# A linear-attention state without zero blocks, its products on 64x64 parts of the array, and a new order of all engines

## The chip, the cores and the metric

The kernel runs on one core of one Trainium2 chip. The metric is the device time of one execution in microseconds (us); lower is better. The engines have names in the profile: PE is TensorE's matmul and PEld its weight load, DVE is VectorE, ACT is ScalarE, POOL is GpSimd, and SP issues the transfers (DMA). Each engine works through its own queue in the order in which the program gave it its instructions, and waits for others by semaphores. TensorE writes into PSUM, which only VectorE and ScalarE read.

## The reference

Two layers. The first is a linear attention with a decaying state, over 4 batches, 8 heads, 768 time steps and a head size of 48; the second is a dense layer with a squared ReLU in its middle, on 3072 tokens of width 384 with a hidden width of 2048.

```python
state = zeros(B, H, D, D)
for t in range(S):
    cur = einsum('bhd,bhe->bhde', u[None] * k[t], v[t])
    y[t] = einsum('bhd,bhde->bhe', r[t], state + cur)
    state = w[t][..., None] * state + einsum('bhd,bhe->bhde', k[t], v[t])
x = y as (3072, 384)
out = (maximum(x @ w_in, 0) ** 2) @ w_out
```

All inputs and the output are in 32-bit floats; w lies between 0.80 and 0.95.

## The kernel before

Time is cut into 12 steps of 256 tokens, three for each batch (`NB = 3`). A step has two chunks c of 128 tokens, and the 128 partitions hold pairs of tokens: rows `c * 64` to `c * 64 + 63` are chunk c, and j = 0 or 1 is the token of a pair. Heads go in four pairs p, with e = 0 or 1 the head of a pair; a head's 48 columns are padded to 64 in the operands of transposes, so that head e of a pair lies on partitions `e * 64` on.

The work of one step s, by the names that the order uses:

- `ld.s.w`, `.r`, `.k`, `.v` load one step's inputs (384 KB each), `ld.g.i` and `ld.g.o` a quarter of w_in and w_out (768 KB each), which `cast.i.g` and `cast.o.g` turn into 16-bit floats.
- `ww_`, `lw_` (logarithm), `cum_` (cumulative sums by a matmul with a triangle), `exp_` give the decays; `ac_` the decay over a whole chunk. `rw_`, `kw_`, `rd_` apply them to r and k.
- `tr_` and `rkt_` transpose these through TensorE and PSUM (steps 0 to 2), `dtr_` by a transposing transfer (steps 3 to 11), into `rkT`.
- `p_` multiplies k and r of the same chunk, `pm_` masks the result.
- `ku_`, `qp_`, `q_`, `vq_` form the term with u, token by token.
- `su_` adds up the chunk's outer products of k and v in PSUM (the state update), `ts_` adds the old state S to it, `sn_` multiplies by the decay and gives the new S.
- `y_` (masked products with v), `yq_` (the term with u) and `yc_` (r with the carried state S) add into one PSUM tile of two banks, bank c for chunk c. `ysb_` copies it out; `yt_` and `xt_` (steps 0 to 3) or `dyt_` (a transposing transfer, steps 4 to 11) turn it into xT.
- `m1_` is x @ w_in in eight groups of six matmuls, `rl_` the ReLU, `sq_` the square. For steps 0 to 4 `m2_` multiplies by w_out in four quarters for each chunk. Steps 5 to 11 use a form with seven products in place of eight: `sw_` and `tw_` add and subtract blocks, `pw_` are the seven products, `cx_` and `ow_` combine them. `os_` scales, `store` writes.

Nothing schedules this but one text, `ORDER` (lines 17 to 91): a list of words, each one operation of one step, executed in that order (lines 638 to 650), so that each engine's queue is the order of its words. A letter behind = says which engine does it (V is DVE, A is ACT, G is POOL), a number behind a colon which PSUM tile it uses. Buffers come from small pools and are free for the next step after a counted number of uses (`uses_of`, `buf`). `warm_` are matmuls on zeros that keep TensorE at work in the opening.

In the state tile S and in PSUM each head pair takes 96 columns on all 128 partitions: rows of head e times columns of both heads. Only the block with the same head is wanted. The other block is computed by `su_` (its matmul takes the weights of both heads and the v of both heads) and is multiplied away in `sn_`, since `ac_` is held with a zero for it: the tile is cleared once (line 275), and two activations fill in each half (lines 360 and 361). So S is zero off the head's own block, and `yc_` can contract over all 128 partitions in one matmul.

The lines that matter: L408 `p_`, L430 `su_`, L438 and L440 `ts_`, L444 `sn_`, L454 the matmuls of `y_`, `yq_` and `yc_` (all issued by `y_mm`), L360 `ac_`, L517 `m1_`, L540 `m2_`, L594 `pw_`, L225 `cast`, L336 to L340 `cum_`.

## Time and profile before

| what | us |
| --- | --- |
| runs | 178.8, 177.38, 178.2 |
| median | 178.2 |
| span of the profiled execution, first to last instruction | 176.7 |
| PE busy in the span | 168.7 |
| DVE busy | 141.4 |
| ACT busy | 135.7 |
| POOL busy | 125.8 |

Of the profiled execution the page gives the span; what the device time holds beyond it is not listed. The page gives busy time, share and number of instructions of each engine, then the busy share over 40 slices of the span as digits (9 is 90% or more). A chain of waits follows the work that ended last back to the start: "DMA" in it is a transfer that was waited for, "SPq" the issuing of transfers, "issue" time without a visible reason. In groups, a row gives line, engine, operation, tiles and shape, the count, then busy us and mean ns of one, then the idle time of the engine before it and what ended that. For a matmul "64*128" is the part of the array that it uses, rows by columns. Matmuls overlap, so a mean duration is longer than the time from one start to the next. In a timeline the columns are start, length and what.

### The profile page before, as it was taken

Reading aid. Unit: us, or ns where it says so; the run is one execution under the profiler, and the core shown is the slowest. Engines: PE = TensorE matmul, PEld = TensorE weight load, DVE = VectorE, ACT = ScalarE, POOL = GpSimd, SP = SyncE. Lnnn points to the kernel's source line nnn. Section 1 sums busy time; section 2 is a strip of 40 time slices with the busy share of each in tenths; the row PEclk is TensorE's granted clock in tenths of the full one; section 3 lists DMA queues with packets and bytes.
Section 4 is the critical chain, followed back from the end, with each engine's and each line's share of the span. In section 5 each row is a group of like instructions: output and inputs, shape, how many; then the busy total and the mean of one; then the engine's idle time right before and its main releaser. Section 6 shows DMA issues by size and latency. Waiting matters only on the chain.

```text
span 176.7 us, 5829 instructions
## 1 busy us (share of the span) xinstructions
PE 168.7 (95%) x2431; PEld 133.3 (75%) x2431; DVE 141.4 (80%) x221; ACT 135.7 (77%) x229; POOL 125.8 (71%) x116
## 2 busy tenths in 40 slices
PE   7969799999999999999999999999999999999993
PEld 2336678866687677578776888889988888989992
DVE  5299976994888968997877979979899879788731
ACT  5677799998659896939899799997897688477320
POOL 6298979999978099969999319759939665165220
DMA  5999999999699999797999959989959930330123
GB/s 142 315 305 340 380 244 347 370 347 254 152 220 240 287 199 254 184 215 179 308 225 194 329 136 222 224 113 269 251 115 132 227 53 4 108 114 4 45 93 134
DMA packets 82667, 36.55 MB, mean 207 GB/s; under 512 B 75857, under 2 KB 81106, under 8 KB 82642
## 3 DMA queue, kind: packets, MB, share of 16 engines
q1 hardware_dynamic: 82642, 36.19, 82.7%
q8 instruction: 19, 0.31, 0.7%
q14 instruction: 6, 0.05, 0.1%
HBM read 25.17 MB, written 4.72 MB: 169 GB/s over the span
## 4 chain that ended last, share of the span: by engine, by line
PE 85%; SPq 6%; DMA 5%; issue 1%; ACT 1%; ACTq 0%
PE one L517 35%; PE one L594 19%; PE one L540 15%; PE att L454 7%; DMA w_st_b<-in_moe_w_in_dram 5%; SPq L205 4%; PE att L408 3%; PE att L430 2%; SPq L213 2%; PE att L338 1%; SPq L233 1%; PE one L500 1%; PE att L340 1%; PE one L383 1%; PE att L336 0%
## 5 line engine op out<-in xcount | busy, mean ns | idle before, releaser
L517 PE MATMUL one<-xT_b,wi_sb 128*128 128x256 bf16 x576 | 70.3, 273 | 0.6 <-ACT gt_b L524 0.4
L517 PEld LDWEIGHTS <-wi_sb 128*128 128x128 f16 x576 | 54.7, 98 | 9.4 <-issue 1.3
L524 ACT ACTIVATE gt_b<-one 128x512 f16<-128x512 f32 x70 | 40.8, 596 | 10.1 <-PE one L517 9.4
L532 ACT ACTIVATE gt_b<-gt_b 128x1024 bf16<-128x1024 f16 x42 | 43.5, 1056 | 1.4 <-DVE gt_b L526 1.0
L419 DVE TENSOR_TENSOR pmT_b<-att,mask 128x1024 bf16<-128x1024 f32 x22 | 26.3, 1217 | 4.2 <-PE att L408 4.2
L540 PE MATMUL one<-wo_sb,gt_b 128*128 128x384 f16 x160 | 28.7, 326 | 0.0
L594 PEld LDWEIGHTS <-gt_b 128*128 128x128 bf16 x280 | 23.2, 98 | 0.9 <-issue 0.4
L311 POOL TENSOR_TENSOR ku_b<-k_b,u_bc 128x768 f32<-128x768 f32 x12 | 22.3, 1862 | 1.0 <-ACT ac_buf L360 0.8
L316 POOL TENSOR_TENSOR ku_b<-ku_b,r_b 128x768 f32<-128x768 f32 x12 | 22.2, 1848 | 0.6 <-DMA r_b<-in_r_dram 0.4
L540 PEld LDWEIGHTS <-gt_b 128*128 128x128 bf16 x160 | 15.1, 98 | 9.6 <-issue 0.5
L444 POOL TENSOR_TENSOR S_b<-t_b,ac_buf 128x384 bf16<-128x384 f32 x20 | 16.9, 846 | 5.4 <-ACT t_b L438 4.8
L526 DVE TENSOR_SCALAR gt_b<-one 128x512 f16<-128x512 f32 x26 | 17.6, 686 | 3.0 <-PE one L517 2.2
L322 POOL TENSOR_TENSOR vq_b<-v_b,q_b 128x768 bf16<-128x768 f32 x12 | 18.2, 1518 | 0.9 <-DVE q_b L319 0.8
L594 PE MATMUL one<-wo_sb,gt_b 128*128 128x192 f16 x168 | 16.2, 246 | 0.0
L374 DVE TENSOR_TENSOR rdec_buf<-r_b,att 128x768 bf16<-128x768 f32 x12 | 11.4, 948 | 1.8 <-POOL r_b L304 0.8
L374 DVE TENSOR_TENSOR rdec_buf<-k_b,att 128x768 bf16<-128x768 f32 x12 | 11.4, 948 | 1.7 <-ACT ac_buf L360 1.1
L319 DVE TENSOR_REDUCE q_b<-ku_b 128x16 f32<-128x768 f32 x12 | 11.3, 944 | 1.7 <-POOL ku_b L316 1.7
L599 ACT ACTIVATE w_st_b<-one 128x192 f32<-128x192 f32 x14 | 4.4, 329 | 10.3 <-PE one L594 10.2
L304 POOL TENSOR_TENSOR r_b<-r_b,w_b 128x384 f32<-128x384 f32 x8 | 8.1, 1014 | 4.7 <-DMA r_b<-in_r_dram 4.7
L292 POOL TENSOR_TENSOR ww_b<-w_b 128x384 f32<-128x384 f32 x7 | 8.0, 1149 | 4.5 <-DMA w_b<-in_w_dram 4.5
L594 PE MATMUL one<-w_st_b,gt_b 128*128 128x192 f16 x112 | 11.2, 246 | 0.0
L440 DVE TENSOR_TENSOR t_b<-S_b,att 128x384 f32<-128x384 bf16 x16 | 8.8, 548 | 2.9 <-POOL S_b L444 2.8
(100 smaller groups left out, 266.5 us busy)
## 6 DMA issues: line engine op xcount, KB each, us to landing
w_b<-in_w_dram SPq DMA_DIRECT2D x12, 384.0 KB, 5.9
r_b<-in_r_dram SPq DMA_DIRECT2D x12, 384.0 KB, 5.4
k_b<-in_k_dram SPq DMA_DIRECT2D x12, 384.0 KB, 5.3
v_b<-in_v_dram SPq DMA_DIRECT2D x12, 384.0 KB, 5.0
out_dram<-w_st_b SPq DMA_DIRECT2D x23, 192.0 KB, 2.2
w_st_b<-in_moe_w_in_dram SPq DMA_DIRECT2D x4, 768.0 KB, 9.5
w_st_b<-in_moe_w_out_dram SPq DMA_DIRECT2D x4, 768.0 KB, 9.1
rkT_b<-rdec_buf SPq DMA_TRANSPOSE x18, 3.5
```

The costliest lines, as they stand in the source:

```text
L311: nc.gpsimd.tensor_mul(buf("ku", s)[:], buf("k", s)[:, :, 1:3, :], u_bc[:, :, None, :].to_broadcast([C, H, 2, D]))
L316: nc.gpsimd.tensor_mul(ku[:], ku[:], buf("r", s)[:, :, 0:2, :])
L322: nc.gpsimd.tensor_mul(buf("vq", s)[:].rearrange("p j h d -> p h j d"), buf("v", s)[:], buf("q", s)[:, :, :, None].to_broadcast([C, H, 2, D]))
L374: nc.vector.tensor_mul(rdec[:, i, :, heads, 0:D], x.rearrange("p h j d -> p j h d"), decay[:, None, :, :].to_broadcast([C, 2, n, D]))
L419: nc.vector.tensor_mul(pmT, ps_p[:].rearrange("p e (a x) -> p (e a) x", a=2), mk.to_broadcast([C, 4, 2 * C]))
L444: nc.gpsimd.tensor_mul(buf("S", s + c, 1 - c)[:], buf("t", s, c)[:].rearrange("p (a e d) -> p a e d", a=HP, e=2), tiles["a_c", s][:, :, c, ...
L517: nc.tensor.matmul(ps1[:, j, :], wi_sb[:, n // 4, kk, n % 4 * 128:(n % 4 + 1) * 128], xT[:, :, kk, :], start=(kk == 0), stop=(kk == KT - 1))
L524: nc.scalar.activation(rl, m1, AF.Relu, scale=RS)
L526: nc.vector.tensor_scalar(out=rl, in0=m1, scalar1=RS, scalar2=0.0, op0=ALU.mult, op1=ALU.max)
L532: nc.scalar.activation(gt, rl, AF.Square)
L540: nc.tensor.matmul(m2, gt[:, n, c * C:(c + 1) * C], wo_sb[:, n, :], start=(n == 0), stop=(n == NT - 1))
L594: nc.tensor.matmul(where_to, gt[:, n, :], wo[:, n, :], start=(n == 0 and i in (1, 2, 5)), stop=(n == NT // 2 - 1), skip_group_check=True)
```

## The change

The state S loses its zero blocks: it is [128, 4, 48] in place of [128, 4, 2, 48], rows e of a pair holding head e alone. `ts_`, `sn_` and the decay tile of `ac_` shrink to that size; `ac_` is one activation, and the clearing of its tile goes.

`su_` issues a matmul for each head e, with 64 rows (chunk c) and 64 columns (head e) of the array, writing 48 columns to partitions `e * 64` on. The carried product can no longer contract over 128 partitions: each head's matmul uses the 64 rows of its e. It is split in halves. `yc_` does the heads with c = e, `yb_` the others, so that within a half each row part of the array writes another PSUM bank. Between the halves stands other work whose matmuls use another part size of the array; in steps 0 and 1 `yd_` takes the second half with 64x32 parts.

The order is new as a whole, for all engines; `ku_`, `qp_`, `vq_` and `sn_` may run on DVE, and in step 0 `rd_`, `tr_`, `rkt_`, `ysb_`, `yt_` and `xt_` come in halves. The diff, cut to its core; of the order only the opening and the end:

```diff
 ORDER = """
-ld.0.w warm_.10.1 ld.1.w ld.0.u ld.0.r ld.0.k ld.1.k ww_.0=V lw_.0 ld.1.r cum_.0:1 ww_.1=V ub_:1 lw_.1 exp_.0 ld.0.v
-rw_.0=G ac_.0 warm_.1.3 uc_=A cum_.1:0 ld.0.i kw_.0=V warm_.4.3 ku_.0 ac_.1 rd_.0.0 exp_.1 ld.1.v rd_.0.1 tr_.0.0:0
-rkt_.0.0=A kw_.1=V ld.1.i tr_.0.1:1 rw_.1=G rd_.1.1 warm_.4.2 ld.2.i rkt_.0.1=A ld.3.i qp_.0 warm_.1.0 rd_.1.0 v_.0=A
-ld.2.w p_.0.0:n pm_.0.0 su_.0:1 tr_.1.1:2 ts_.0.0=A q_.0 p_.0.1:0 rkt_.1.1=A sn_.0.0 warm_.4.0 pm_.0.1 ld.2.k
...
+ld.0.k ld.0.w ww_.0=V warm_.6.1 ld.0.u ld.0.r ld.1.w warm_.3.1 lw_.0 kw_.0=G ld.1.k ub_:3 ld.1.r uc_=V cum_.0:0
+ku_.0=V warm_.4.2 ld.0.v exp_.0 rw_.0=V rd_.0.1.1 tr_.0.1.1:1 rkt_.0.1.1=A qp_.0=G ld.1.v rd_.0.0.1 tr_.0.0.1:0 ld.2.w
+rkt_.0.0.1=A warm_.4.2 ww_.1=G rd_.0.1.0 rd_.0.0.0 p_.0.1:1 ac_.0 ld.2.i kw_.1=G q_.0 tr_.0.1.0:2 lw_.1 tr_.0.0.0:0
+cum_.1:0 pm_.0.1 rw_.1=G warm_.1.1 warm_.8.3 ld.1.i ld.0.i rkt_.0.1.0=A ac_.1 ku_.1=V ld.3.i vq_.0=G exp_.1 ld.2.k
+v_.0=A rd_.1.0 rkt_.0.0.0=A su_.0:1 ld.2.r p_.0.0:n ts_.0.0=A tr_.1.0:3 rd_.1.1 v_.1=A sn_.0.0=G qp_.1=G rkt_.1.0=A
+tr_.1.1:2 yd_.0:0 yq_.0 rkt_.1.1=A pm_.0.0 q_.1 ts_.0.1=V y_.0 yc_.0 cast.i.2=G ysb_.0.0=A p_.1.1:n ysb_.0.1=A
+yt_.0.0:3 xt_.0.0=A yt_.0.1:2 pm_.1.1 sn_.0.1=G ww_.2=G p_.1.0:0 su_.1:1 xt_.0.1=A cast.i.1=A m1_.0.5:3 m1_.0.4:0
+pm_.1.0 vq_.1=G lw_.2 ts_.1.0=V m1_.0.2:1 rl_.0.5=A sn_.1.0=V cum_.2:0 rl_.0.4=A m1_.0.3:3 ts_.1.1=V rl_.0.2=A exp_.2
+ld.2.v sn_.1.1=V y_.1:1 rl_.0.3=A yq_.1 yc_.1 yd_.1 cast.i.0=V ld.0.o m1_.0.1:2 ysb_.1=A cast.i.3=V m1_.0.0:3
...
+sw_.10.1.3=G sq_.11.0=A sw_.9.1.4=V sw_.9.0.4=V cx_.10.1=V pw_.9.7 pw_.9.3 pw_.10.6 sw_.11.1.1=V ow_.10.1=V sq_.11.1=A
+ow_.9.4=V pw_.9.4 ow_.9.2=V sw_.10.1.4=V sw_.10.0.4=V ow_.9.3=A cx_.10.2=A store.9.0 store.3.0 pw_.10.5 sw_.11.1.2=G
+store.9.1 sw_.11.0.1=G pw_.11.1:0 pw_.11.2:3 cx_.10.3=A sw_.11.1.4=V cx_.11.1=A pw_.10.7 pw_.10.3 ow_.11.1=V
+ow_.10.2=V store.10.0 sw_.11.0.3=G sw_.11.0.2=G pw_.11.6 sw_.11.1.3=G ow_.10.4=V pw_.11.5 cx_.11.2=A sw_.11.0.4=G
+pw_.10.4 cx_.11.3=V pw_.11.7 ow_.10.3=V store.10.1 pw_.11.3 ow_.11.4=V pw_.11.4 store.11.1.1 ow_.11.2=V store.11.0
+warm_.1.5 ow_.11.3=V store.11.1.0
 """
...
-        rkT=(2, [C, 2, 2, HP, C], BF16), pmT=(2, [C, 2, 4, 2, C], BF16), t=(2, [C, DM], FP32),
-        S=(6, [C, HP, 2, D], BF16), y_sb=(2, [C, 2, DM], BF16), xT=(4, [C, 2, KT, C], BF16),
+        rkT=(2, [C, 2, 2, HP, C], BF16), pmT=(2, [C, 2, 4, 2, C], BF16), t=(2, [C, HP * D], FP32),
+        S=(6, [C, HP, D], BF16), y_sb=(2, [C, 2, DM], BF16), xT=(4, [C, 2, KT, C], BF16),
...
-        for e in range(2):
-            rows = slice(e * DP, (e + 1) * DP)
-            nc.scalar.activation(
-                a_c[rows, :, :, e], cs[rows, 0, DM:DM + 2 * HP].rearrange("p (a c) -> p a c", c=2), AF.Exp)
+        nc.scalar.activation(a_c[:], cs[:, 0, DM:DM + 2 * HP].rearrange("p (a c) -> p a c", c=2), AF.Exp)
...
         for j in range(2):
             for p in range(HP):
-                for c in range(n_c):
-                    part = slice(c * Q, (c + 1) * Q)
-                    nc.tensor.matmul(ps_su[c][:, p * 2 * D:(p + 1) * 2 * D],
-                                     rdec[part, 1, j, 2 * p:2 * p + 2, :], v_bf[part, 2 * p:2 * p + 2, j, :],
-                                     start=(j == 0 and p == 0), stop=(j == 1), skip_group_check=True)
+                for e in range(2):
+                    for c in range(n_c):
+                        part = slice(c * Q, (c + 1) * Q)
+                        nc.tensor.matmul(ps_su[c][e * DP:(e + 1) * DP, p * D:(p + 1) * D],
+                                         rdec[part, 1, j, 2 * p + e, :], v_bf[part, 2 * p + e, j, :],
+                                         start=(j == 0 and p == 0), stop=(j == 1), skip_group_check=True)
...
-        nc.gpsimd.tensor_mul(buf("S", s + c, 1 - c)[:],
-                             buf("t", s, c)[:].rearrange("p (a e d) -> p a e d", a=HP, e=2),
-                             tiles["a_c", s][:, :, c, :, None].to_broadcast([C, HP, 2, D]))
+        product("sn_", s, c)(buf("S", s + c, 1 - c)[:],
+                             buf("t", s, c)[:].rearrange("p (a d) -> p a d", a=HP),
+                             tiles["a_c", s][:, :, c, None].to_broadcast([C, HP, D]))
...
+    def carried(s, swap, size):
+        rkT, first = buf("rkT", s), 0 if s % NB else 1
+        S = {c: buf("S", s, c) for c in range(first, 2)}
+        for p in range(HP):
+            for j in range(2):
+                for e in range(2):
+                    c, rows, h = e ^ swap, slice(e * DP, (e + 1) * DP), 2 * p + e
+                    if c in S:
+                        for at in range(0, Q, size):
+                            y_mm(s, c, slice(h * D, (h + 1) * D),
+                                 rkT[rows, 0, j, p, c * Q + at:c * Q + at + size], S[c][rows, p, :], j, at)
...
     def yc_(s):
-        rkT = buf("rkT", s)
-        for c in range(0 if s % NB else 1, 2):
-            S_c = buf("S", s, c)
-            for p in range(HP):
-                for j in range(2):
-                    y_mm(s, c, slice(2 * p * D, (2 * p + 2) * D), rkT[:, 0, j, p, c * Q:(c + 1) * Q],
-                         S_c[:, p].rearrange("p e d -> p (e d)"), j)
+        carried(s, 0, Q)
...
+    def yb_(s):
+        carried(s, 1, Q)
...
+    def yd_(s):
+        carried(s, 1, Q // 2)
```

203 lines of the change are left out of this document (101 added, 102 removed).

## The prediction

> **What bounds the kernel now.** I read the page first, then the busy time by stretches, then the chain of waits in order of time.
>
> ```profile
> span 176.7 us, 5829 instructions
> PE 168.7 (95%) x2431; PEld 133.3 (75%) x2431; DVE 141.4 (80%) x221; ACT 135.7 (77%) x229; POOL 125.8 (71%) x116
> PE   7969799999999999999999999999999999999993
> PE 85%; SPq 6%; DMA 5%; issue 1%; ACT 1%; ACTq 0%
> ```
>
> ```profile
> core 0: us, PE busy (x) PEld busy (x) DVE busy (x) ACT busy (x) POOL busy (x), PEclk, DMA share, GB/s
> 0.00:23.30 23.30, 18.27 (x240) 10.54 (x241) 17.53 (x29) 16.77 (x29) 17.16 (x29) 1.00 0.98 298
> 23.30:173.50 150.20, 150.19 (x2191) 122.79 (x2190) 123.87 (x193) 118.57 (x199) 108.66 (x88) 1.00 0.82 194
> ```
>
> ```profile
> 22.66 0.60 ACT gt_b L524
> 23.27 0.04 issue
> 23.31 0.82 PE one L517 x6
> ...
> 153.12 6.55 PE one L517 x60
> 159.67 13.88 PE one L594 x168
> ...
> 173.62 0.33 ACT w_st_b L599
> ```
>
> The span has three parts. Up to 23.3 us TensorE is fed by loads (DMA share 0.98). From 23.3 to 173.5 it is busy for 150.19 of 150.20 us at clock 1.00; the next busiest engine, DVE, works 123.87 of them. Then come one copy and the last store. In the middle part only two things count: how long TensorE's own instructions take, and whether something else begins to make it wait. The sum is made on this execution, whose span is 176.7 us; the median of the runs shown is 178.2, so I add 1.5 us for what lies around the span.
>
> **What the small matmuls cost.** These are TensorE's instructions around one step's output (y_, yc_, yq_, then m2_), one state update, and a place where yq_ is followed by p_ of the same array shape. The columns are start, length to the last end, and what; lengths overlap, so I take start to start.
>
> ```profile
> 40.70 0.57 PE L454 MATMUL att<-v_bf_b,pmT_b 64*128 64x48 bf16 x32
> 41.20 0.53 PE L454 MATMUL att<-S_b,rkT_b 128*64 128x96 bf16 x16
> 41.66 0.36 PE L454 MATMUL att<-vq_b,ident 64*64 64x384 bf16 x4
> 41.95 0.50 PE L540 MATMUL one<-wo_sb,gt_b 128*128 128x384 f16 x2
> ...
> 48.44 0.51 PE L430 MATMUL att<-v_bf_b,rdec_buf 64*128 64x96 bf16 x16
> 48.89 0.39 PE L517 MATMUL one<-xT_b,wi_sb 128*128 128x256 bf16 x2
> ```
>
> ```profile
> 17.30 0.36 PE L454 MATMUL att<-vq_b,ident 64*64 64x384 bf16 x4
> 17.49 0.39 PE L408 MATMUL one<-rkT_b 64*64 64x128 bf16 x16
> 17.71 0.39 PE L408 MATMUL att<-rkT_b 64*64 64x128 bf16 x16
> ```
>
> yq_ takes 41.95 - 41.66 = 0.29 us when another shape follows, but 17.49 - 17.30 = 0.19 when p_ with the same 64*64 shape follows. A change of shape thus costs 0.10 us. The 16 matmuls of p_ after it take 17.71 - 17.49 = 0.22 with no change behind them: four parts of the array side by side, so 4 rounds of 0.055. Taking the change off the others: y_ is 0.50 - 0.10 = 0.40 for 32 matmuls, two side by side, so 16 rounds of 48 columns at 0.025; yc_ is 0.46 - 0.10 = 0.36 for 8 rounds of 96 columns, about 0.044; su_ is 48.89 - 48.44 - 0.10 = 0.35 for 8 rounds, 0.044.
>
> **State update and carried product on 64x64 parts.** su_ becomes 32 matmuls of 48 columns, four side by side: again 8 rounds, but of 48 columns. In the last step of each batch it works on one row half, 16 matmuls, two side by side, 8 rounds, as its 8 matmuls did 8 rounds before. So su_ is 12 x 8 = 96 rounds before and after. yc_ before is 8 rounds in eight steps and 4 in the four steps that begin a batch: 80. After, yc_ and yb_ (or yd_) are 4 rounds each in every step: 96. Before: 176 rounds x 0.044 = 7.7 us. After: 192 rounds of a shape, 48 columns on 64x64 parts, that no row shows. It lies between the round of y_ (same 48 columns, 0.025: 4.8 us) and that of yc_ (96 columns, 0.044: 8.4 us), so the change is between -2.9 and +0.7 us. What could hold it up is the loading of weights, which for column halves seems slower:
>
> ```profile
> L454 PEld LDWEIGHTS <-pmT_b 64*128 64x128 bf16 x384 | 5.7, 93 | 2.2 <-issue 1.6 <-DVE pmT_b L419 0.2 <-DVE w_st_b L572 0.2
> L454 PEld LDWEIGHTS <-rkT_b 128*64 128x64 bf16 x160 | 4.1, 109 | 1.0 <-issue 0.6
> L408 PEld LDWEIGHTS <-rkT_b 64*64 64x64 bf16 x384 | 6.0, 106 | 3.3 <-issue 2.2 <-ACT rkT_b L388 0.6 <-DVE t_b L440 0.3
> ```
>
> A load of 64 columns shows 106 to 109 ns where one of 128 shows 93. I read the excess, 0.013 to 0.016 us, as load time, hidden under 96 or 128 columns but perhaps only partly under 48. I stay near y_'s row and give the new round 0.029, for its columns are the same: 192 x 0.029 = 5.6, a gain of 2.1 us. A group that now begins with the slower load shows the excess once, 22 groups (su_ 12, yb_ 10) x 0.013 = 0.3 us back.
>
> The Trainium skill speaks against this edit: "TensorEngine Tiling (Array Packing)", section "Restrictions and Gotchas", says that column tiling excludes fast weight load, and "TensorE: Matmul & The Clock Gate", section "LDWEIGHTS (loading the stationary operand)", gives columns / 1.2 in ns, 53 ns for 64 columns. An estimate by these is 192 rounds x 0.053 = 10.2 us, 2.5 more than before. The trace agrees with slower loads of column halves but not with that size: yc_, with such loads in each round, already goes at 0.044.
>
> **Changes of shape and the wait between the halves.** yc_ had a shape of its own; it now has that of yq_, and often of p_ or su_ beside it. Against that yb_ is a separate group, parted from yc_ by y_ or other matmuls of another shape; in steps 0 and 1, where nothing lies between, yd_ on 64x32 parts makes the change itself. Counting along the two orders I get 87 changes before and 86 after: -0.1 us. The wait is this change of shape: what queues behind it is only TensorE's own stream, and its 0.10 us is in the count. TensorE in all: -2.1 + 0.3 - 0.1 = -1.9 us.
>
> **Half the state elsewhere.**
>
> ```profile
> L444 POOL TENSOR_TENSOR S_b<-t_b,ac_buf 128x384 bf16<-128x384 f32 x20 | 16.9, 846 | 5.4 <-ACT t_b L438 4.8
> L440 DVE TENSOR_TENSOR t_b<-S_b,att 128x384 f32<-128x384 bf16 x16 | 8.8, 548 | 2.9 <-POOL S_b L444 2.8
> L360 ACT ACTIVATE ac_buf<-att 64x8 f32<-64x8 f32 x24 | 4.1, 172 | 2.8 <-PE att L340 2.3 <-PE att L338 0.2
> L374 DVE TENSOR_TENSOR rdec_buf<-r_b,att 128x768 bf16<-128x768 f32 x12 | 11.4, 948 | 1.8 <-POOL r_b L304 0.8
> L572 POOL TENSOR_TENSOR gt_b<-gt_b 128x512 bf16<-128x512 bf16 x3 | 3.5, 1152 | 3.6 <-DVE sg_b L572 3.5
> ```
>
> ts_ and sn_ work on 192 columns in place of 384, ac_ is one instruction in place of two (12 x 0.172 = 2.1 us off ACT). sn_ at half of 0.846 and 8 of 20 on DVE takes about 12 us off POOL; half of ts_ takes at most 16 x 0.27 = 4.4 us off DVE. The new order then moves ten products of 128x768 (four ku_, three qp_, three vq_) from POOL to DVE, some 10 x 0.95 = 9.5 us by L374's row, and 16 combination products sw_ from DVE to POOL, 16 x 1.15 = 18 us there. In SP's queue loads, stores and transposes keep their numbers and change places. All this lies beside TensorE: three engines that work 109 to 124 of 150 us can each change by 10 us and stay under it, so I cost it at nothing. If the cover fails in one place, its price is that wait; this is a rival below.
>
> **The opening.** What makes m1_ wait there is w_in.
>
> ```profile
> 19.98 2.93 PE L517 MATMUL one<-xT_b,wi_sb 128*128 128x256 bf16 x24 [0.20 <-DVE xT_b L504]
> ...
> 15.87 1.48 ACT L225 CAST wi_sb<-w_st_b 128x1536 f16<-128x1536 f32 x1 [0.33 <-DMA w_st_b<-in_moe_w_in_dram]
> 19.25 1.47 ACT L225 CAST wi_sb<-w_st_b 128x1536 f16<-128x1536 f32 x1 [0.48 <-DMA w_st_b<-in_moe_w_in_dram]
> 21.29 1.47 ACT L225 CAST wi_sb<-w_st_b 128x1536 f16<-128x1536 f32 x1 [0.57 <-DMA w_st_b<-in_moe_w_in_dram]
> ```
>
> ```profile
> w_b<-in_w_dram SPq DMA_DIRECT2D x12, 384.0 KB, 5.9
> ...
> w_st_b<-in_moe_w_in_dram SPq DMA_DIRECT2D x4, 768.0 KB, 9.5
> ```
>
> Each cast starts as its load lands. Until 15.87 seven loads of 384 KB and one of 768 had come, 3456 KB; until 19.25, 1152 KB more (341 KB/us); until 21.29, 768 more (376 KB/us). The new order loads nine of 384 KB (v of step 1 and w of step 2 moved ahead) and then w_in's third, second, first and fourth quarter. By these rates they land at 15.87 + 768/341 = 18.1, 19.25 + 384/376 = 20.3, 22.3 and 24.4. With a cast of 1.5 us m1_ starts at 19.6 in place of 19.98, does two groups of six (0.66 us each, by the 60 matmuls in 6.55 us of the chain above), waits from 20.9 to 21.8 for the second quarter, and goes on. Before, 0.6 us went by in the same place (22.66 to 23.27 in the chain). The first group starts 0.4 earlier and the waits are 0.3 longer; but y_ and the small work of steps 1 and 2 stand in the gap while the last two quarters come, which I value at 0.2. I take 0.3 us gained, between 1.0 lost and 1.5 gained.
>
> Sum: 176.7 - 1.9 - 0.3 = 174.5 us of span; with 1.5 around it, **176.0 us**. The tail (last copy, last store) stays as it is.
>
> **Rivals.** First, loads of 64-column weights set the round. For it: 106 to 109 ns against 93. Against it: p_ goes four side by side at 0.055 for 128 columns with no loss. It gives +0.7 for the rounds, +0.3, -0.1 and -0.3 from the opening: 178.8. Chance 0.16. It is this case that the two pages named above would make; by the page's 53 ns it would be 180.6.
>
> Second, TensorE gets its work done sooner and is then left waiting inside: by POOL, whose sw_ products take 1.15 us each, six of them for the last step alone behind one another (6.9 us), or by DVE. For it: before, TensorE's slack was used to the last 0.01 us. Against it: the state chain su_, ts_, sn_ is shorter. One to two us of the gain lost: 177.5. Chance 0.08.
>
> Third, and slower: the casts of the first and fourth quarter of w_in now stand in DVE's queue, behind the work of both first steps.
>
> ```profile
> L308 DVE TENSOR_TENSOR k_b<-k_b,w_b 128x384 f32<-128x384 f32 x6 | 4.5, 752 | 2.5 <-DMA k_b<-in_k_dram 2.5
> ...
> L504 DVE COPY xT_b<-one 128x768 bf16<-128x768 bf16 x4 | 2.2, 554 | 0.4 <-PE one L500 0.4
> ...
> L388 DVE COPY rkT_b<-one 128x1024 bf16<-128x1024 bf16 x3 | 2.1, 688 | 0.4 <-PE one L383 0.4
> ```
>
> DVE worked 17.5 of the first 23.3 us. There come to it two ku_ and one rw_ (3 x 0.95, the rw_ at most that), u's copy (0.5), two sn_ (0.4 each) and the two casts (1.5 each as on ACT, or 1.9 as twice L374's row): 7.2 us. Two kw_, one rkt_ and one xt_ leave it: 2.7. That makes 22.0 us of work by about 25.9, when the fourth quarter's cast (24.4 + 1.5) is due, so 3.9 us are left for waiting where 5.8 were. TensorE has nothing else to do there, so each us of delay is one of the total; five us late gives 181. It decides from a cast that ends at 29.9 on, since the gain of 2.2 goes first and 1.8 more makes 1%. Chance 0.08.
>
> Fourth, the opening gains the full 1.5 and the rounds reach 0.025: 176.0 - 1.2 - 0.8 = 174.0. Chance 0.08.
>
> **How the numbers follow.** The three runs spread from 177.38 to 178.8, so about 1% (176.4 and 180.0) is what can be told from no change. My forecast has a chance of 0.60 and its own range of 174.9 to 177.1 from the bounds of opening and rounds; three quarters of that lie under 176.4. Faster: 0.45 + 0.08 = 0.53. Within 1%: 0.15 + 0.14 + 0.07 = 0.36. Slower: 0.08 and the ends of the others, 0.11. The range of 8 in 10 takes in the fourth case in part and the first two: 174.2 to 178.9.
>
> **What would show it.** TensorE's rows: su_ start to start near 0.33 in place of 0.45, yc_ followed by yq_ near 0.12 and no gap between, yb_ with its change near 0.22. Busy time of PE from the first m1_ to the end lower by about 2 us. First m1_ near 19.6. If su_ stays at 0.45, the loads set the round. If PE shows idle time after 26 us, the second rival is at work, and if the cast of the fourth quarter ends after 28, the third.

## The result: slower, and where the profile after shows it

| kernel | runs | median (us) | from to |
| --- | --- | --- | --- |
| before | 4 | 178.37 | 177.38 to 178.8 |
| changed | 4 | 185.03 | 184.48 to 185.44 |

The ratio is 1.0395, with a 95% interval of 1.0351 to 1.0439: the change makes the kernel 4% slower, where 176.0 us was forecast. The chip has a slower state into which some runs, and the profiled executions marked with * below, fall: medians and ranges are over all runs, ratios and intervals leave the slow ones out, and where the two disagree the ratio counts.

The page of the changed kernel, the same rows as before:

```profile
span 183.4 us, 6501 instructions
PE 172.4 (94%) x2777; PEld 134.6 (73%) x2777; DVE 154.8 (84%) x230; ACT 128.4 (70%) x214; POOL 127.7 (70%) x112
PE   7999699999999997998999999999988899999992
PEclk9999789999999999999999999999999999999999
PE 73%; DVE 14%; DMA 6%; issue 3%; ACT 1%; SPq 0%; ACTq 0%; DVEq 0%
```

The span grew by 6.7 us. The chain that ended last was 85% PE before and is 73% PE now; DVE, which was not in it, holds 14%. The page now has a row of the granted clock (PEclk), with a 7 and an 8 in it; the page before has none, and its stretches read 1.00. The busy times in three stretches, first before, then changed (columns as in the prediction: from:to, length, then busy time and number of instructions of each engine, clock, DMA share, GB/s):

```profile
20.00:26.00 6.00, 5.61 (x89) 4.32 (x89) 4.70 (x7) 5.18 (x6) 4.92 (x5) 1.00 1.00 292
60.00:100.00 40.00, 40.00 (x583) 29.50 (x581) 32.89 (x40) 33.06 (x57) 35.73 (x29) 1.00 1.04 230
100.00:146.00 46.00, 46.00 (x764) 40.43 (x765) 41.03 (x70) 39.42 (x72) 31.57 (x26) 1.00 0.89 180
```

```profile
20.00:26.00 6.00, 4.92 (x73) 3.89 (x73) 4.56 (x8) 3.72 (x6) 3.34 (x3) 0.72 1.04 313
60.00:100.00 40.00, 38.08 (x666) 28.12 (x659) 36.59 (x49) 28.34 (x47) 30.52 (x24) 1.00 0.98 201
100.00:146.00 46.00, 43.17 (x829) 36.67 (x827) 44.81 (x64) 36.27 (x62) 36.36 (x30) 1.00 0.89 188
```

TensorE used to be busy for every hundredth between 60 and 146 us. Now it is idle for 1.92 + 2.83 = 4.75 us there, while DVE works 44.81 of 46 us; and around 20 us the mean clock is 0.72. TensorE's waits by what they waited for (us in total, times, longest):

```profile
PE att L410 <- issue: 1.5, 1, 1.5
PE att L460 <- DVE pmT_b L421: 1.3, 1, 1.3
...
PE one L538 <- ACT w_st_b L567: 0.7, 1, 0.7
PE att L433 <- DVE rdec_buf L376: 0.6, 1, 0.6
PE att L460 <- DVE t_b L443: 0.6, 1, 0.6
```

Most of them are for DVE. The first has no releaser at all ("issue"): it lies in the opening, inside a group of p_, whose operands were there:

```profile
19.29 0.30 PE L410 MATMUL att<-rkT_b 64*64 64x128 bf16 x5
21.08 0.53 PE L410 MATMUL att<-rkT_b 64*64 64x128 bf16 x11 [1.49 <-issue]
21.30 0.72 PE L433 MATMUL att<-v_bf_b,rdec_buf 64*64 64x48 bf16 x32
21.96 3.15 PE L538 MATMUL one<-xT_b,wi_sb 128*128 128x256 bf16 x18
```

The small matmuls themselves did become faster. Rows of su_ and of a yc_ with a wide group behind it:

```profile
46.02 0.31 PE L460 MATMUL att<-S_b,rkT_b 64*64 64x48 bf16 x16
46.27 2.77 PE L561 MATMUL one<-wo_sb,gt_b 128*128 128x384 f16 x16
...
49.31 0.44 PE L433 MATMUL att<-v_bf_b,rdec_buf 64*64 64x48 bf16 x32
49.68 0.82 PE L561 MATMUL one<-wo_sb,gt_b 128*128 128x384 f16 x4
```

Start to start su_ takes 0.37 (0.45 before), a half of the carried product 0.25. With 0.10 for the change of shape the new round is (0.37 - 0.10) / 8 = 0.034 and (0.25 - 0.10) / 4 = 0.038 us.

The account, from the first m1_ to the last matmul (19.98 to 173.37 before, 21.96 to 179.82 after), all from start to start, and waits taken off the kinds. Counted so, a wait has the tail of the matmul ahead of it in it: 6.1 us, where the idle time behind the first m1_ is 4.74 (0.39 before).

| term | us |
| --- | --- |
| first m1_ later (of it 1.49 the wait without a releaser) | +2.0 |
| ten m1_ matmuls at 0.213 in place of 0.109 | +1.0 |
| waits of TensorE behind it, 6.1 against 0.6 | +5.5 |
| su_, carried product, yq_, y_, p_: 21.1 against 23.2 | -2.1 |
| tail | +0.3 |
| sum, against 6.7 of span | +6.7 |

So the gain that was forecast is there in TensorE's stream behind the first m1_, and three losses that were not are laid over it. The experiments ask for the cause of each.

### The profile page after: what moved, and what is told of

Read it like the earlier page. It is cut to its first block, busy times and chain, and to the rows that moved or that the text cites. A ratio compares the mean times of both kernels' runs of the same rounds, so it can differ in the third digit from the quotient of the medians.

```text
span 183.4 us, 6501 instructions
## 1 busy us (share of the span) xinstructions
PE 172.4 (94%) x2777; PEld 134.6 (73%) x2777; DVE 154.8 (84%) x230; ACT 128.4 (70%) x214; POOL 127.7 (70%) x112
## 4 chain that ended last, share of the span: by engine, by line
PE 73%; DVE 14%; DMA 6%; issue 3%; ACT 1%; SPq 0%; ACTq 0%; DVEq 0%
PE one L538 25%; PE one L561 14%; PE one L615 13%; PE att L460 5%; PE one L643 5%; DVE pmT_b L421 4%; DMA rkT_b<-rdec_buf 4%; PE att L410 3%; DMA out_dram<-w_st_b 2%; PE one L385 2%; PE att L433 2%; DVE rdec_buf L376 2%; DVE gt_b L593 1%; DVE v_bf_b L305 1%; PE att L343 1%
## 5 line engine op out<-in xcount | busy, mean ns | idle before, releaser
L327 POOL TENSOR_TENSOR vq_b<-v_b,q_b 128x768 bf16<-128x768 f32 x9 | 14.6, 1623 | 9.1 <-DVE q_b L324 6.7
L321 POOL TENSOR_TENSOR ku_b<-ku_b,r_b 128x768 f32<-128x768 f32 x9 | 16.9, 1874 | 2.0 <-DVE ku_b L316 2.0
L316 POOL TENSOR_TENSOR ku_b<-k_b,u_bc 128x768 f32<-128x768 f32 x8 | 15.2, 1899 | 2.7 <-DMA k_b<-in_k_dram 2.7
L309 POOL TENSOR_TENSOR r_b<-r_b,w_b 128x384 f32<-128x384 f32 x9 | 11.5, 1273 | 7.6 <-DMA r_b<-in_r_dram 7.6
L593 POOL TENSOR_TENSOR gt_b<-gt_b 128x512 bf16<-128x512 bf16 x11 | 13.8, 1257 | 3.9 <-DVE sg_b L593 3.7
L447 POOL TENSOR_TENSOR S_b<-t_b,ac_buf 128x192 bf16<-128x192 f32 x12 | 7.8, 650 | 8.6 <-ACT att L358 3.8
L358 ACT ACTIVATE att<-att 128x768 f32<-128x768 f32 x12 | 9.6, 801 | 5.6 <-PE att L345 3.1
L510 ACT CAST y_sb_b<-att 128x768 bf16<-128x768 f32 x10 | 8.0, 796 | 5.5 <-PE att L460 5.4
L376 DVE TENSOR_TENSOR rdec_buf<-k_b,att 128x768 bf16<-128x768 f32 (+1 forms) x13 | 11.5, 883 | 0.2
L376 DVE TENSOR_TENSOR rdec_buf<-r_b,att 128x768 bf16<-128x768 f32 (+1 forms) x13 | 11.5, 884 | 0.0
```

The lines of the kernel that those rows point to most:

```text
L316: product("ku_", s)(buf("ku", s)[:], buf("k", s)[:, :, 1:3, :], u_bc[:, :, None, :].to_broadcast([C, H, 2, D]))
L321: product("qp_", s)(ku[:], ku[:], buf("r", s)[:, :, 0:2, :])
L327: product("vq_", s)(buf("vq", s)[:].rearrange("p j h d -> p h j d"), buf("v", s)[:], buf("q", s)[:, :, :, None].to_broadcast([C, H, 2, D]))
L376: nc.vector.tensor_mul(rdec[:, i, :, heads, 0:D], x.rearrange("p h j d -> p j h d"), decay[:, None, :, :].to_broadcast([C, 2, n, D]))
L593: engine_of("sw_", s, h, i).tensor_tensor(out=out, in0=x, in1=y, op=op)
```

## Experiments: which part of the change

**The new parts alone**: the changed kernel's operations under the order and the choice of engines of the kernel before. Since in this order y_ stands directly ahead, the second half is always `yd_`.

```diff
-y_.1:1 rl_.0.0=V yc_.1 ld.3.k ww_.2=G yq_.1
+y_.1:1 rl_.0.0=V yd_.1 yc_.1 ld.3.k ww_.2=G yq_.1
```

> The state without zero blocks and all 64x64 parts, in the order and with the engines of the kernel before; yd_ stands directly ahead of yc_ in each step, its 64x32 parts being the wait between the halves. Theory A (the order with its choice of engines costs the time, the parts themselves save): TensorE saves about 0.07 us in each of 12 su_ and nearly nothing in yc_, DVE saves 16 x 0.2 us and POOL 20 x 0.35 us beside it; 176.5 to 178.5 us and no wait of TensorE over 0.2 us after 24 us. Theory B (the parts themselves cost it, by twice the small instructions of TensorE, their loading or their draining): 182 us or more.

Measured: 182.07 us (181.02 to 182.36, 4 runs), ratio 1.0221 (1.0177 to 1.0265). DVE is at 138.0 us and TensorE's stretch behind the first m1_ is as long as before (153.44 against 153.39 us), but that m1_ starts at 22.51. So this loss lies in the opening, in the new parts with the old order too. Behind that point the parts gain nothing: their small matmuls take 0.9 us less, from start to start, but seven m1_ matmuls at half clock (0.7 us) and 0.5 us more of waits give it back.

**The new order alone**: the changed kernel's order and engines, with the state, su_ and the carried product of before.

```diff
     def su_(s):
...
-                for e in range(2):
-                    for c in range(n_c):
+                for c in range(n_c):
...
     def yb_(s):
-        carried(s, 1, Q)
+        pass
-    def yd_(s):
-        carried(s, 1, Q // 2)
+    yd_ = yb_
```

> The new order and engines with the state, su_ and yc_ of the kernel before (zero blocks, whole columns, one yc_ in place of the two halves). Theory A: the waits after 65 us stay and TensorE has some 2.5 us more to do, and sn_ and ts_ are twice as large on DVE; 185 to 189 us. Theory B: 178 to 181 us.

Measured: 185.6 us (183.9 to 187.87, 4 runs; profile *), ratio 1.0351 (1.03 to 1.0403). The order alone loses nearly all that the change loses, but in part elsewhere. It has no wait without a releaser near 20 us. Its sn_ on DVE have twice the size, and two casts of w_in queue behind them; that is the third rival of the prediction, at 2.42 us:

```profile
25.00 2.03 DVE L451 TENSOR_TENSOR S_b<-t_b,ac_buf 128x384 bf16<-128x384 f32 x1
26.95 4.23 DVE L232 CAST wi_sb<-w_st_b 128x1536 f16<-128x1536 f32 x2
```

```profile
28.76 2.56 PE L535 MATMUL one<-xT_b,wi_sb 128*128 128x256 bf16 x12 [2.42 <-DVE wi_sb L232]
```

**Order and choice of engines crossed**: the changed kernel with the letters of before in the new order, and the new parts in the old order with the new letters.

```diff
-ld.0.k ld.0.w ww_.0=V warm_.6.1 ld.0.u ld.0.r ld.1.w warm_.3.1 lw_.0 kw_.0=G
+ld.0.k ld.0.w ww_.0=V warm_.6.1 ld.0.u ld.0.r ld.1.w warm_.3.1 lw_.0 kw_.0=V
```

> The changed kernel with its sequence, but each of the 149 operations that changed engine put back on the engine it had before. Theory A1 (the choice of engines is what costs: products on DVE and sw_ on POOL get into each other's way and fill DVE): 177 to 180.5 us, DVE busy under 147 us. Theory A2 (the sequence costs: it asks for results too early): 183 us or more. Theory B: 183 us or more.

> As e1, but with the engines of the changed kernel for each operation that both orders have: sequence of before, 149 operations on other engines. Theory A1: DVE busy over 151 us, waits of TensorE after 60 us, 181 us or more. Theory A2: within 1.5 us of e1. Theory B: 182 us or more, as e1.

Measured: 200.58 us (ratio 1.1272, 1.122 to 1.1324) and 200.64 us (1.1274, 1.1232 to 1.1317). Both are far worse than either parent. They fall into the open ends ("183 us or more", "181 us or more") of theories that expected no such size. A likely reading, which no run tests, is that order and letters were fitted to each other, so that one cannot be judged without the other. They tell nothing of the cause.

## Experiments: the opening

TensorE's instructions come by transfers of their own. The page gives them one row ("q8 instruction: 21, 0.34, 0.8%" after, 19 before); the trace has the times of each, 16384 bytes every time. A wait without a releaser falls behind 446 TensorE records (loads and matmuls), and ends soon after the landing of one of these transfers:

```
kernel                   record 190   transfer          record 446 runs   wait ahead
before                   14.45        17.68 to 18.64    20.78             none
changed                  14.92        18.70 to 19.63    21.08             1.49
parts alone              14.89        18.34 to 19.45    20.81             0.95
```

The wait ends 1.36 to 1.45 us after the landing. Before, the same record was due only when TensorE had gone on to the wide m1_ groups: its first m1_ is record 430 or so, against 527 and 530 with the new parts. The theory: TensorE reads its instructions in blocks of 16 KB, 256 records; the transfer of the next block starts some time after one block is done, and twice as many matmuls for the same work read a block out before the next has come.

**More instructions ahead in the kernel before**: each warming matmul cut into three.

```diff
-            nc.tensor.matmul(one[i][:] if i < 4 else att[i - 4][:, 0, :], warm[:, 0:C], warm[:], start=True, stop=True)
+            for cols in (slice(0, 171), slice(171, 342), slice(342, 512)):
+                nc.tensor.matmul((one[i][:] if i < 4 else att[i - 4][:, 0, :])[:, cols], warm[:, 0:C], warm[:, cols],
+                                 start=True, stop=True)
```

> The kernel before, with each warm_ matmul of 512 columns issued as three of 171, 171 and 170: the same columns, 48 more pairs of weight load and matmul ahead of the first m1_ (527 instructions in place of 430). Theory C (code: the first piece of TensorE's instructions ends after 446 weight loads and matmuls, the next is usable some 1.4 us after its transfer lands, about 20 us; who gets there earlier waits, and the idle time halves the clock for 3.4 us): a wait with no releaser at record 446, cadence 0.213 us of the first m1_ matmuls in place of 0.109, 180 to 182.5 us. Theory D (the opening of the two slower kernels is late for their data, and the clock by chance): 177.5 to 179 us, no such wait.

Measured: 177.87 us (10 runs), ratio 0.9979 (0.9948 to 1.0009): no loss, against the theory as I had put it. The trace shows why: record 190 was already reached at 12.12, so the transfer came earlier too (15.24 to 16.20), and TensorE paused for only 0.17 us there, again until 1.28 us after the landing. The 256 records took 4.97 us to read, against 4.45 in the changed kernel with its wait of 1.49 and 6.33 before with none. What counts is how fast one block is read, not how many instructions stand ahead.

**The dense part of the opening moved behind the first m1_ group**, in the parts alone and in the changed kernel:

```diff
-p_.1.0:0 su_.1:1 xt_.0.1=A cast.i.1=A m1_.0.5:3 m1_.0.4:0
+xt_.0.1=A cast.i.1=A m1_.0.5:3 p_.1.0:0 su_.1:1 m1_.0.4:0
```

> As e1, but p_.1.0 and su_.1 moved behind the first group of m1_, so that 430 instructions of TensorE stand ahead of it, as in the kernel before. Theory C: no wait without releaser before the first m1_, no half clock, TensorE's stream from the first m1_ on shorter by 2 to 2.6 us; 175.5 to 177.5 us, faster than both kernels. Theory D: within 1 us of e1's 182.1. Theory B (the parts cost it later): 180 us or more.

> The changed kernel with the same move: p_.1.0 and su_.1 behind the first group of m1_ (434 instructions ahead of it in place of 530). Theory C: first m1_ about 20 us, its matmuls at 0.109, 1.5 to 3.3 us off: 181.7 to 183.5 us; the waits after 60 us stay. Theory D: 184.5 to 185.5 us.

Measured: 180.84 us (ratio 1.0132, 1.0071 to 1.0192) and 184.07 us (1.0305, 1.0238 to 1.0372), each about 1 us better and neither as good as expected. The first m1_ does start early (19.41 and 19.64), and the clock stays full; in the changed kernel it has already waited 1.1 us for POOL's cast of w_in. But the wait for instructions comes back further on, in the parts alone:

```profile
23.98 0.27 PE L458 MATMUL att<-S_b,rkT_b 64*32 64x48 bf16 x25
25.46 0.45 PE L458 MATMUL att<-S_b,rkT_b 64*32 64x48 bf16 x23 [1.20 <-issue]
```

and in the changed kernel, 1.74 us:

```profile
24.23 0.42 PE L460 MATMUL att<-S_b,rkT_b 64*64 64x48 bf16 x19
26.39 0.30 PE L460 MATMUL att<-S_b,rkT_b 64*32 64x48 bf16 x29 [1.74 <-issue]
```

Both stand at record 702, which is 446 + 256, and both end 1.4 us after the next transfer (23.07 to 24.08 and 23.95 to 24.97). That fits the block: 16384 bytes by 256 records are 64 bytes each. In the parts alone these 256 records take 5.3 us with the wait, in the changed kernel 6.2.

**Longer work in the second block**: two more m1_ groups ahead of the carried product of step 1 in the changed kernel, one in the parts alone.

```diff
-sn_.1.1=V y_.1:1 rl_.0.3=A yq_.1 yc_.1 yd_.1 cast.i.0=V ld.0.o m1_.0.1:2 ysb_.1=A cast.i.3=V m1_.0.0:3
+sn_.1.1=V cast.i.0=V m1_.0.1:2 rl_.0.3=A cast.i.3=V m1_.0.0:3 y_.1:1 yq_.1 yc_.1 yd_.1 ld.0.o ysb_.1=A
```

> The changed kernel with the shifted opening of the earlier run (184.07 us), and two of the first projection's groups (24 wide matmuls, about 2.6 us) moved ahead of the carried product of step 1, so that the TensorE instructions between records 446 and 702 take longer. Theory I (TensorE's instructions arrive in blocks of 16 KB, 256 records; a block read in less than about 6 us leaves TensorE waiting for the next): the wait of 1.9 us at record 702 falls below 0.4 us, and the time to 181.9 to 182.8. Rival (that wait is on data of the carried product, and moves along with it): the wait stays at 1.5 us or more in front of the same operation, and the time stays at 183.5 to 184.5.

> The new parts alone with the shifted opening (180.84 us, with a wait of 1.2 us for instructions at record 702), and one more group of the first projection (12 wide matmuls, 1.3 us) ahead of the carried product of step 1. Theory I: the wait at record 702 is gone and the time is 179.2 to 180.2; what is left above the kernel before is then under 1%. If the new parts cost time by themselves: 180.5 us or more with no wait at record 702. If they gain what the prediction's TensorE term said (1.9 us): below 178.

Measured, changed kernel: 187.33 us (185.41 to 189.67, 4 runs), ratio 1.0478 (1.041 to 1.0546). The wait at record 702 is gone, as the theory has it, but the time went up, outside of what both sides expected: the groups that were moved up now wait for the cast of w_in, and ysb_ comes late for yt_:

```profile
25.51 1.48 PE L538 MATMUL one<-xT_b,wi_sb 128*128 128x256 bf16 x12 [0.96 <-DVE wi_sb L232]
...
29.17 0.51 PE L520 MATMUL one<-ident,y_sb_b 128*128 128x128 bf16 x6 [1.00 <-ACT y_sb_b L510]
```

Parts alone: 180.93 us (179.13 to 186.89, 6 runs), ratio 1.0106 (1.0046 to 1.0165). Its wait at record 702 fell from 1.20 to 0.24 us in the profiled execution, which took 179.13, but the median did not fall below that of the run without the edit. Whether a rest of 1% belongs to the parts themselves stays open; that they gain 1.9 us in this order is refuted.

**The block by itself**: in the kernel before, four warming matmuls ahead of the first m1_ are replaced by 48 small ones of about the same 0.9 us.

```diff
     def warm_(n, i):
+        if (n, i) == (4, 0):
+            for m in range(48):
+                rows, part = slice(m % 2 * DP, m % 2 * DP + DP), slice(m // 2 % 2 * Q, m // 2 % 2 * Q + Q)
+                nc.tensor.matmul(one[m % 2][part, m // 4 % 4 * C:m // 4 % 4 * C + C], warm[rows, 0:Q], warm[rows, 0:C],
+                                 start=True, stop=True)
+            return
         for _ in range(n):
```

> The kernel before, with its last four warming matmuls of 512 columns ahead of the first projection replaced by 48 small ones on 64x64 parts that take about as long (0.9 us): 88 more instructions in the same TensorE time. Theory I: record 446 now comes before the first projection starts, while the transfer of the next block still begins about 3.2 us after record 190; TensorE waits for it about 1 us, the first matmul of the projection is 1 us later, and the time is 179.4 to 181.5. Rival (the number of instructions does not matter): 177.9 to 178.9, with no wait at record 446.

Measured: 180.28 us (179.91 to 183.53, 5 runs), ratio 1.0122 (1.0079 to 1.0165). The kernel before got 88 more records in about the same TensorE time (48 pairs of load and matmul in place of four), and there are the same wait and the same half clock (profile *):

```profile
19.45 0.22 PE L408 MATMUL att<-rkT_b 64*64 64x128 bf16 x1
21.33 0.64 PE L408 MATMUL att<-rkT_b 64*64 64x128 bf16 x15 [1.66 <-issue]
21.90 0.82 PE L500 MATMUL one<-ident,y_sb_b 128*128 128x128 bf16 x6
22.66 0.82 PE L430 MATMUL att<-v_bf_b,rdec_buf 64*128 64x96 bf16 x16
23.41 0.82 PE L517 MATMUL one<-xT_b,wi_sb 128*128 128x256 bf16 x3
```

The transfer ran from 18.90 to 19.85, and record 190 at 15.77, so the 256 records were read in 3.6 us. A row of p_, in which the changed kernel stalled too, stalls here, with the old state and the old order. Of the 3.4 us by which the first m1_ is later, 1.66 are this wait; 1.3 were lost ahead of record 190 in this execution. This settles the cause of the wait: it is the number of instructions per time. It does not say that a kernel is back at its old time once the wait is gone; the two runs ahead of it were not.

## Experiments: DVE and POOL

Between 60 and 146 us the trace of the changed kernel shows DVE instructions that last far longer than their like. From the changed kernel, DVE and then POOL:

```profile
131.35 1.92 DVE L593 TENSOR_TENSOR w_st_b<-gt_b 128x512 bf16<-128x512 bf16 x1
...
139.37 1.20 DVE L447 TENSOR_TENSOR S_b<-t_b,ac_buf 128x192 bf16<-128x192 f32 x1
140.60 0.35 DVE L443 TENSOR_TENSOR t_b<-S_b,att 128x192 f32<-128x192 bf16 x1
140.87 1.65 DVE L593 TENSOR_TENSOR gt_b<-gt_b,w_st_b 128x512 bf16<-128x512 bf16 x1
...
143.84 0.34 DVE L447 TENSOR_TENSOR S_b<-t_b,ac_buf 128x192 bf16<-128x192 f32 x1
...
144.71 0.42 DVE L593 TENSOR_TENSOR gt_b<-gt_b,w_st_b 128x512 bf16<-128x512 bf16 x1
```

```profile
131.19 1.80 POOL L321 TENSOR_TENSOR ku_b<-ku_b,r_b 128x768 f32<-128x768 f32 x1
...
139.20 1.15 POOL L593 TENSOR_TENSOR sg_b<-gt_b 128x512 bf16<-128x512 bf16 x1
140.31 1.93 POOL L316 TENSOR_TENSOR ku_b<-k_b,u_bc 128x768 f32<-128x768 f32 x1
```

The same sn_ takes 0.34 us at 143.84, with POOL idle, and 1.20 at 139.37; the same sum 0.42 and 1.65. Each long one starts while a POOL instruction runs and ends 0.2 to 0.3 us after it: 133.27 behind 132.99, 140.57 behind 140.35, 142.52 behind 142.24. t_b at 140.60, with one of its two inputs in PSUM, runs beside POOL at its usual 0.35.

This holds for all of them. In the seven kernels compared below, 108 DVE instructions took over 0.15 us more than the shortest of their kind, 22 of them in the changed kernel (15.6 us in sum). Every one began beside a POOL instruction and ended behind that one's end by a time that only its own form sets, within 0.01 us: 0.22 us for an sn_ of 192 columns, 0.28 for a sum of 512, 0.42 for a product of 384 or a cast of 768, 0.82 for a product of 768 or a cast of 1536. So a DVE sum or product with both inputs in SBUF, or a cast from SBUF to SBUF, that comes behind a POOL instruction waits until that one is through and does nearly all of its work only then (alone, the sn_ takes 0.34 us and the sum 0.42), and all that queues behind it on DVE stands too. Upstream the cast of v for step 6, which the new order gives to DVE, shows how TensorE pays (DVE, then TensorE):

```profile
69.69 2.13 DVE L305 CAST v_bf_b<-v_b 128x768 bf16<-128x768 f32 x1
71.74 1.21 DVE L421 TENSOR_TENSOR pmT_b<-att,mask 128x1024 bf16<-128x1024 f32 x1
```

```profile
73.01 0.57 PE L460 MATMUL att<-v_bf_b,pmT_b 64*128 64x48 bf16 x32 [1.26 <-DVE pmT_b L421]
```

The Trainium skill has this as a rule: "SBUF — State Buffer", section "Who interferes with whom", says that DVE and GpSimd share one pair of ports as an exclusive lock; that a DVE instruction with two inputs in SBUF contends with a GpSimd instruction that reads SBUF; and that in DVE's modes of two ports, which a cast can enter, whoever issues first has the pair for the whole instruction while the other blocks fully. The rows agree, with the numbers above; in which mode the casts ran is not shown.

To measure it, I add up, over all DVE instructions, the time above the shortest one of the same operation, operands and shape among seven kernels (before, changed, the parts alone, and the four edits below). It is 9.2 us before, 8.6 with the parts alone, and 17.9 in the changed kernel. Of these 17.9, 7.8 fall on work that DVE did not have before: sn_, ku_, qp_, vq_ and three casts.

A rival would be that POOL's own results come late. But DVE waits for results of POOL for 6.0 us before and for 0.7 in the changed kernel, and POOL is not in the chain that ended last.

Four edits take work from one side or the other; each leaves out part of the computation. The first makes the sums that POOL does for the last product (`sw_`) for a quarter of their blocks:

```diff
+        if where["sw_", s, h, i] == "G" and (i > 2 or s >= 7):
+            out, x, y = out[:, 0:1], x[:, 0:1], y[:, 0:1]
         engine_of("sw_", s, h, i).tensor_tensor(out=out, in0=x, in1=y, op=op)
```

> The changed kernel, POOL's sw_ (the third and fourth form in all steps, all four from step 7 on) done on a quarter of their elements, so that POOL works some 20 us less; the rest of the output is wrong data. Theory A (POOL and DVE in each other's way): DVE's products with both operands in SBUF come back to their shortest times, DVE busy falls by 4 us or more from 154.8, TensorE's waits after 60 us (6.1 us in sum) fall to 3 or less, 181 to 183 us. Rival (DVE simply has too much work, POOL has no part in it): DVE busy falls by under 2 us, 184 us or more.

The second makes DVE's ku_, qp_ and vq_ from step 3 on for one of the eight heads (the expectation says twelve, which is a slip):

```diff
+        n = heads_of("ku_", s)
-        product("ku_", s)(buf("ku", s)[:], buf("k", s)[:, :, 1:3, :],
-                             u_bc[:, :, None, :].to_broadcast([C, H, 2, D]))
+        product("ku_", s)(buf("ku", s)[:, 0:n], buf("k", s)[:, 0:n, 1:3, :],
+                             u_bc[:, 0:n, None, :].to_broadcast([C, n, 2, D]))
```

> The changed kernel, where those products of r, k, u and v that VectorE makes from step 3 on are made for one head of twelve only: some 6 us less work on VectorE, none of it moved. If VectorE's total work is what keeps TensorE waiting between 70 and 146 us: the waits there fall from about 4.5 us to under 2, and the time to 181.5 to 183.5. If it is the waiting of single VectorE instructions behind GpSimd's: the waits fall by less than 1.5 us, and the time is 183.8 to 185.

The third makes all of POOL's products from step 6 on for one of eight heads, its sn_ for one of four pairs, and its sw_ for a quarter (the fractions in the expectation are slips of the same kind). The fourth does this for the products alone, with sn_ and sw_ whole.

```diff
     def product(*word):
-        return nc.vector.tensor_mul if where[word] == "V" else nc.gpsimd.tensor_mul
+        if where[word] == "V":
+            return nc.vector.tensor_mul
+        if word[1] >= 6:
+            return lambda out, x, y: nc.gpsimd.tensor_mul(out[:, 0:1], x[:, 0:1], y[:, 0:1])
+        return nc.gpsimd.tensor_mul
```

> The changed kernel, where GpSimd makes only a twelfth of each head-wise product, a sixth of each state update from step 6 on, and a quarter of most of its sums of the last product: VectorE's work stays as it is, GpSimd is nearly idle after 80 us. If VectorE's instructions are held up by GpSimd's in flight: VectorE's time above the shortest of each form falls from 17 us to under 9, TensorE's waits between 80 and 146 us from about 4.5 us to under 2, and the time to 181 to 183. If VectorE's total work is what counts: the waits fall by less than 1.5 us, and the time is 183.8 to 185.

> The changed kernel, where GpSimd's products over heads from step 6 on are made for one head, while its state updates and all its sums of the last product stay whole. If the products hold VectorE up: most of the gain of the run with all pieces comes back, 182 to 183.3 us. If the moved sums and updates do: 184.2 to 185.2 us. If only all of them together: in between, 183.3 to 184.2.

Measured (the third column is the sum just defined, the fourth TensorE's idle time from 60 to 146 us by the view of stretches, the fifth its idle time behind the first m1_):

| kernel | median us, ratio (interval) | DVE above shortest | PE idle 60 to 146 | PE idle behind first m1_ |
| --- | --- | --- | --- | --- |
| before | 178.37 | 9.2 | 0.0 | 0.4 |
| changed | 185.03, 1.0395 (1.0351 to 1.0439) | 17.9 | 4.75 | 4.7 |
| POOL's sums on a quarter * | 185.17, 1.0352 (1.0266 to 1.0437) | 16.0 | 4.6 | 4.6 |
| DVE's products on one head * | 186.55, 1.0384 (1.0336 to 1.0432) | 19.7 | 3.0 | 4.8 |
| POOL's products on one head | 182.67, 1.0214 (1.0139 to 1.029) | 11.6 | 2.05 | 2.3 |
| all three of POOL on pieces | 181.85, 1.0202 (1.0148 to 1.0256) | 8.8 | 0.8 | 1.1 |

The last one's stretches:

```profile
60.00:100.00 40.00, 39.45 (x705) 29.08 (x704) 36.54 (x51) 29.83 (x49) 17.43 (x26) 1.00 0.95 213
100.00:146.00 46.00, 45.72 (x886) 39.16 (x884) 42.23 (x68) 38.01 (x65) 18.85 (x35) 1.00 0.93 195
```

DVE's own work is untouched in it, and its time above the shortest is back to that of the kernel before; 3.2 us come off, though the opening's loss is still in it. Taking work from DVE itself gained nothing: its ratio of 1.0384 is that of the changed kernel within the intervals, and TensorE's idle time behind its first m1_ is 4.8 us as before the edit. The 3.0 from 60 to 146 us is smaller only because that execution began 1.4 us later, which moved most of the last wait (0.85 us, up to 146.56) out of the stretch. Taking only the sums from POOL gained nothing clear either (1.0352, as that run's rival had it), so the 18 us of moved `sw_`, which the prediction had watched, are not what hurts by themselves. What does is POOL's long products over heads, 1.6 to 1.9 us each in the mean: with them alone made for one head, nearly all of the gain is there (1.0214 against 1.0202). POOL has fewer of them than before, 26 where it had 36; what is new is the DVE work that the order sets beside them.

**Both causes attacked at once**: the shifted opening and POOL on pieces together, in the changed kernel.

> The changed kernel with the shifted opening (184.07 us) and with GpSimd on pieces as in the run before it (181.85 us). If the late block and GpSimd's hold on VectorE are two separate causes: the gain of the pieces (about 3.2 us) comes on top of the shifted opening, 180 to 181.2 us, with the block wait of about 1.9 us at record 702 still in it, so that without that wait it would be near the kernel before. If the two overlap: 181.5 us or more.

Measured: 180.65 us (179.85 to 184.43, 4 runs; profile *), ratio 1.0107 (1.0046 to 1.0167), inside the range for two separate causes. What is left, 1.1% or 2 us, has the size of the wait at record 702, 1.78 us in its profile, that this opening still holds. That it is this wait is not shown: the two runs that took it away gained no time.

## Why the prediction was wrong, step by step

- **Rounds of the small matmuls** (forecast 0.029, bounds 0.025 and 0.044): measured 0.034 to 0.038. The gain of this term was forecast too large by some 0.007 x 192 = 1.3 us, but fewer changes of shape are paid than the count of 86 said: yq_ fell from 3.15 to 1.88 us in all. The sum for TensorE, -1.9 over all steps, came out at -2.1 behind the first m1_, so the size is right in part by two errors that cancel. That balance holds only in the new order; in the old one it is -0.9.
- **The first rival**, loads of 64 columns that set the round, did not come true: the rounds measure 0.034 to 0.038. By the pages of the Trainium skill named there the estimate was 192 x 0.053 = 10.2 us for su_ and the carried product; over the whole execution they take 4.06 + 4.16 + 0.48 = 8.7 us, with their changes of shape.
- **"All this lies beside TensorE ... so I cost it at nothing"** is the step that failed. It compared total times of engines, 109 to 124 of 150 us. But a DVE instruction that comes behind one of POOL's waits it out (0.34 us became 1.20, 0.42 became 1.65), and one that stands still holds back the pm_ or rd_ behind it. Price: 5.5 us of waits, of which most went with POOL's work cut to pieces (idle time from 4.7 to 1.1 us, 3.2 us off the time). The second rival named the place ("by DVE") with a price of one to two us and a chance of 0.08; the mechanism that the price needed was not in it.
- **The opening** (-0.3, bounds -1.5 and +1.0) failed on something that no row of the kernel before made visible: its instruction transfers were there (18.64 landed, 20.78 needed), with 0.7 us to spare by the 1.4 us that follow a landing. The loads themselves came much as forecast (the first two casts of w_in started at 17.90 and 19.77, forecast 18.1 and 20.3). But the first m1_ came at 21.96, not 19.6, with 1.49 us of it the wait for instructions, and ten of them ran at half clock: +3.0 against before.
- **The third rival**, the casts of w_in late on DVE, did not happen in the changed kernel: the last ended at 27.8 us, just below the 28 that the prediction set, and TensorE did not wait for it. With the larger state in the same order it did, for 2.42 us.
- **The tail** stayed within 0.3 us.

## What to carry to other kernels

When a change cuts matmuls into more and smaller ones, count instructions per time as well as rounds: where 256 TensorE records (loads and matmuls) are read in less than 5 to 6 us with busy queues (4.97 us cost 0.17 of wait here, 4.45 cost 1.49), look for waits without a releaser and for the landing of the instruction transfer ahead of them. When work moves between DVE and POOL, the sum of busy times is not enough: list which DVE instructions have both inputs in SBUF or cast from SBUF to SBUF, and what POOL runs beside them, above all ahead of what TensorE needs next. An order taken over under another choice of engines can be far worse than either (200.6 us for both crossings).

## What the runs showed of the hardware that was not expected

- TensorE's instruction transfers are 16 KB for 256 records. Over the kernels here, the one for record 446 starts 3.1 to 4.1 us after record 190 was run, takes 0.9 to 1.1 us, and a TensorE that waits goes on 1.25 to 1.54 us after it. What starts the transfer is not shown.
- A wait of 0.95 to 1.66 us for instructions near 20 us was followed by m1_ at 0.213 in place of 0.109 us in all seven kernels that had one; a wait of 0.45 us once was and once was not. Nor need it be a wait for instructions: in the new order with the old letters, m1_ ran at 0.213 behind a wait of 0.84 us for ysb_. In the changed kernel the clock of 0.72 over 6 us is (1 - 0.72) x 2 x 6 = 3.4 us at one half. The traces' records of the granted clock agree: the pieces at one half last 3.41 us (20.65 to 24.06 in the changed kernel) or 6.83, and two in one execution start a whole multiple of 3.41 us apart (8.54 and 29.02 with the shifted opening and POOL on pieces). The Trainium skill, "TensorE: Matmul & The Clock Gate", Part 1, gives half clock after an idle window of about 3.4 us, and full clock after a busy one of that length. The 3.4 us at one half agree with the second; the waits that were followed by half clock are much shorter than the first. The waits of 1.20 and 1.74 us at record 702, up to 25.46 and 26.39 us, with more wide matmuls ahead of them, were not followed by any loss of clock; the like wait of 1.78 us, up to 27.63, in the run with the shifted opening and POOL on pieces was, from 29.02 on. What tells these apart is open.
- A cast of 128x1536 takes 0.95 us on DVE with POOL out of the way and 2.58 behind POOL's instructions; ACT's takes 1.48.
- A DVE instruction that POOL holds up ends 0.11 to 0.82 us behind POOL's, by its form alone, in 108 cases out of 108.
